# Routing of a mixture of experts behind an attention: smaller steps, another share of them per unit, and the last eight units as one group

## The chip, the core and the metric

The kernel runs on one core of one Trainium2 chip. TensorE (PE in the profile) multiplies matrices, VectorE (DVE), ScalarE (ACT) and GpSimd (POOL) work on tiles in SBUF and PSUM, and SyncE (SP) starts most of the DMAs. Each engine works off its own instructions in the order in which the program wrote them, and waits on semaphores for the others. The metric is the device time of one execution in microseconds.

## The reference, cut to what matters

An mLSTM-like attention over 4 batches, 8 heads, 768 positions and head size 40 gives 3072 rows of 320 numbers. A router picks two of eight experts for each row, and each expert is two matrix products with a maximum between them.

```python
x = attn_out.transpose(0, 2, 1, 3).reshape(3072, 320)
noisy = x @ w_gate + log1p(exp(x @ w_noise)) * noise
top2 = argpartition(-noisy, 2, axis=1)[:, :2]
w = exp(top2_l - top2_l.max()); w /= w.sum() + 1e-9
for e in range(8):
    for k in range(2):
        mask = top2[:, k] == e
        out[mask] += w[mask, k, None] * (maximum(x[mask] @ w1[e], 0) @ w2[e])
```

## The kernel before, in words

**The attention.** The time axis is cut in chunks of 64. A unit is one chunk of two batches with all heads, so there are 24 units (`NU`) of 128 rows. The main loop writes unit after unit by hand, with parts of the neighbours between: at the top the DMAs (`load_unit(i + 3)`, `keep_rows(i - 1)`, which stores the rows of the unit before, `gate_move`, a piece of the first expert's weights), then `k_part(i + 1)` and `p_part(i + 1)` (kd and p, two products on VectorE), `c_part(i)` and `o_part(i)` (TensorE: the state "st" and the output "o"), `e_part(i + 2)`, `f_part(i)` (VectorE: three steps dn and then tm, which read the bank "o"; GpSimd: xr, the unit's rows), logits and transposes of the units before (`l_part`, `t_part`), `s_part(i + 2)` and `sig_part(i + 1)` (ScalarE). There is one bank "o", so the next `o_part` waits for tm. xr also reads the output gate in the unit's input buffer, of which there are four, so SP's load of unit i + 3 waits for GpSimd's xr of unit i - 1.

**The routing.** Four units make a group (`GROUPS`). `g_part(g)` is a generator which writes one group's routing in small steps: logits with noise (two activations on ScalarE between), maxima and their indices (mx, mi), one-hot rows (oh), counts (m, base), then it asks for ranks (`want`), which TensorE adds up with three small products in `r_part`, and turns rank and expert into a place in a table. The place is written as two factors, oa (which of 56 columns) and ob (which of 128 rows), one ob per unit and choice; a burst of matmuls oa by ob in `b_part` adds the tokens' numbers to the table TBL. `decode` reads token numbers out of it, and `gather` fetches rows by them with indirect DMAs that GpSimd issues. Two small tables go on beside: WTS (weights of the two choices, stored behind the rows by a DMA on SP, `sent`) and OVM (for the case that an expert gets too many tokens, which these inputs don't reach).

**How the steps are shared out.** `fill(n)` writes the next n steps of the first group in the queue `routing`; a step that has to wait for another engine ends the fill. RATE gives three steps behind p and five at the unit's end (five and eight from unit 16), and `f_part` calls `fill` once behind each dn. `act()` writes the activations that the routing asked for.

**The first expert.** Its first tokens (places 0 to 511) come from units 0 to 15 alone: as soon as the bursts of four groups are done, the first 4 columns are decoded and four gathers start, beside unit 23. W1 of expert 0 is split in a high and a low half in the attention (`split_w1`: ScalarE w1h, VectorE w1l, line L142) at units 8, 10, ... 18. After the units, `mm1(0, 0, f)` makes eight first products of 512 tokens (banks s0, s1, e in turn; ScalarE hh and VectorE hlo empty each), with w2's split beside (w2h on ScalarE, w2l on GpSimd) and sixteen stores of zeros to the output (`wipe`). `push()` writes all the routing steps that can be written; the ranks and bursts of the last two groups stand between the products: ranks behind f = 0, a burst behind f = 3, ranks behind f = 5. Then `mm2` makes the second products of four tiles of 128 tokens, eight steps of three matmuls each; behind the sixth step of the first tile stand the last burst, the decode of the whole table and seven gathers, three of them for the rest of expert 0, whose transposes (L734) follow the four tiles. The experts 1 to 7 follow, TensorE's work throughout.

Of the kernel before, what the change touches and what calls it, by code (L numbers as in the profile page):

```python
# [8 lines left out]
FR = mybir.dt.float32r  # L9
# [12 lines left out]
NU = 2 * NCH  # L22
# [10 lines left out]
GROUPS = tuple((u, 4) for u in range(0, 24, 4))  # L33
GOF = {u: g for g, (u0, n) in enumerate(GROUPS) for u in range(u0, u0 + n)}
NB = 4

RATE = ((16, (3, 5)), (NU, (5, 8)))
# [14 lines left out]
C_ID, C_TRI, C_ONE, C_I8, C_TOK, C_N, C_SGN, C_VAC, C_END = 0, 128, 256, 384, 392, 416, 544, 592, 648  # L52


def at(plan, i):

    return next(v for end, v in plan if i < end)
# [3 lines left out]
def build(ctx, tc, qk, vk, fi, noise, wgn, w1, w2, cst, ce, out):  # L61
# [403 lines left out]
    acc, bump = {}, {}  # L465
# [6 lines left out]
    OB = rt.tile([128, 8, 128], FR, name="ob", bufs=1)  # L472
    OA = rt.tile([128, 8, NE * TC], FR, name="oa", bufs=1)

    def g_part(g):
# [39 lines left out]
        for j in range(nb):  # L515
            V.max(mx[:, j, :], nl[:, j, :])
            yield
        for j in range(nb):
            V.max_index(mi[:, j, :], mx[:, j, :], nl[:, j, :])
            yield  # L520
# [5 lines left out]
        yield  # L526
        oh4 = sm("oh", [128, nb, 2, NE])
        i8 = cs[:, None, None, C_I8:C_I8 + 8].to_broadcast([128, nb, 2, NE])
        V.tensor_tensor(oh4, i8, e12[:, :, :, None].to_broadcast([128, nb, 2, NE]), op=OP.is_equal)
        yield  # L530

        m = sm("m", [128, NE, nb + 1], BF)
        V.tensor_add(m[:, :, 1:].rearrange("p e u -> p u e"), oh4[:, :, 0], oh4[:, :, 1])
        if u0 == 0:
            V.memset(m[:, :, 0], 0.0)
# [9 lines left out]
        V.tensor_scalar(dd, d, 1.0, 1e-9, op0=OP.add, op1=OP.add)  # L545
# [4 lines left out]
        wt = WTS[:, u0:u0 + nb, 0:2]  # L550
        V.reciprocal(wt[:, :, 0], dd)
        yield
        V.tensor_mul(wt[:, :, 1], d, wt[:, :, 0])
# [20 lines left out]
        r = sm("r", [128, nb, 2])  # L574
        V.tensor_reduce(f(r), oh4.rearrange("p u k e -> p (u k) e"), AX.X, OP.add)
        yield
        ov = sm("ov", [128, nb, 2])
        ix = rt.tile([128, 2 * nb], I32, name=f"ix{u0}", bufs=1)
        V.tensor_scalar(ov, r, float(BLK), None, op0=OP.is_ge)
        V.scalar_tensor_tensor(r, e12, float(BLK), r, op0=OP.mult, op1=OP.add)  # L580
        yield
        V.scalar_tensor_tensor(ix, f(ov), 1e6, f(r), op0=OP.mult, op1=OP.add)
        V.tensor_mul(OVM[:, u0:u0 + nb, 2:4], wt, ov)
# [6 lines left out]
        V.scalar_tensor_tensor(bi, ai, -128.0, ix, op0=OP.mult, op1=OP.add)  # L590
# [575 lines left out]
```

## Time and profile before

| what | value |
|---|---|
| median of 3 runs | 584.05 us (583.41 to 586.16) |
| the profiled execution | 586.08 us, its span 584.2 us |
| busy: PE, DVE, ACT, POOL | 553.9, 360.8, 254.7, 217.2 us |
| mean granted TensorE clock | 0.948 |
| first product of the first expert | at 164.05 us |
| transposes of its second part | at 202.20 us |

A row of the timeline gives start, length, engine, source line, operation, output and inputs with their shape, the number of merged instructions, and in brackets how long the engine idled before it and what released it. Where several instructions are merged the length runs from the first one's start to the last one's end. A row of the windows gives busy times and counts of each engine in a stretch.

### The profile page before, as it was taken

The page shows a single profiled execution, that of the slowest core. Times are in us where ns is not written, and L with a number is a line of the kernel's source. Part 1 is how long each engine was busy: PE and PEld are TensorE (multiplying, and loading weights), DVE is VectorE, ACT ScalarE, POOL GpSimd, SP SyncE. Part 2 cuts the span into 40 slices and gives each one's busy share as a digit, 9 for nine tenths or more (in the row PEclk, how much of TensorE's full clock was granted, in tenths as well). Part 3 has the DMA queues.
Part 4 walks back from the last instruction along what each step waited for, and adds up shares of the span by engine and source line. Part 5 has one row for each costly group of instructions (what it writes and reads, how often), then busy time and mean ns, then how long its engine had stood idle before and what let it go on. Part 6 is the DMA issues. An engine that isn't in the chain of part 4 may idle for free.

```text
span 584.2 us, 13335 instructions
## 1 busy us (share of the span) xinstructions
PE 553.9 (95%) x5157; PEld 506.1 (87%) x5158; DVE 360.8 (62%) x990; ACT 254.7 (44%) x621; POOL 217.2 (37%) x276
## 2 busy tenths in 40 slices
PE   7899979898898999999999999999999999999995
PEld 3687878787776998899899999989989998998995
DVE  8899977898879147663565466356446636645511
ACT  6687848565424234541452254145235315513500
POOL 7355532111423464424604522460451344142043
PEclk9699969796778989999999999999999999999998
DMA  5888875675235956326426442632643343332024
GB/s 142 205 224 220 214 204 145 185 186 166 80 116 186 313 97 140 91 83 148 92 90 146 63 131 43 138 84 90 148 82 116 93 78 82 98 45 24 2 28 48
DMA packets 41060, 71.08 MB, mean 122 GB/s; under 512 B 8761, under 2 KB 30478, under 8 KB 40992
## 3 DMA queue, kind: packets, MB, share of 16 engines
q1 hardware_dynamic: 29632, 51.20, 30.3%
q0 software_dynamic: 11360, 18.98, 19.2%
q8 instruction: 42, 0.69, 0.5%
q14 instruction: 26, 0.21, 0.1%
HBM read 52.73 MB, written 17.73 MB: 121 GB/s over the span
## 4 chain that ended last, share of the span: by engine, by line
PE 70%; DVE 6%; ACT 3%; issue 2%; another core or an unknown queue 1%; DMA 1%; POOL 0%; POOLq 0%; DVEq 0%; ACTq 0%
PE s L871 21%; PE e L871 11%; PE st L890 5%; PE st L889 5%; PE st L891 5%; PE o L891 4%; PE o L890 4%; PE o L889 4%; PE s L734 3%; PE o L365 1%; PE o L898 1%; PE o L897 1%; DVE ob L600 1%; DVE p L342 1%
## 5 line engine op out<-in xcount | busy, mean ns | idle before, releaser
L915 POOL DMA_INDIRECT y_out<-y,tok x56 | 87.1, 1556 | 220.1 <-DVE y L905 219.3
L871 PE MATMUL s<-xh,w1h 128*128 128x512 f32 (+1 forms) x255 | 77.5, 359 | 1.8 <-DVE xh L738 1.2
L877 DVE SCALAR_TENSOR_TENSOR hlo<-s,hh 128x512 fp32r<-128x512 f32 (+1 forms) x85 | 47.4, 558 | 39.8 <-ACT hh L876 37.6
L736 ACT ACTIVATE xh<-s 128x384 fp32r<-128x384 f32 (+1 forms) x56 | 25.6, 470 | 105.3 <-PE s L734 104.6
L704 POOL DMA_INDIRECT xg<-rows,tok x56 | 57.4, 1024 | 25.3 <-issue 18.0
L876 ACT ACTIVATE hh<-s 128x512 fp32r<-128x512 f32 (+1 forms) x85 | 41.8, 492 | 49.2 <-PE s L871 41.2
L871 PE MATMUL s<-xh,w1l 128*128 128x512 f32 (+1 forms) x255 | 63.2, 357 | 0.0
L889 PE MATMUL st<-w2h,hh 128*128 128x320 f32 x184 | 58.3, 317 | 0.0
L890 PE MATMUL st<-w2l,hh 128*128 128x320 f32 x184 | 57.3, 312 | 0.0
L891 PE MATMUL st<-w2h,hlo 128*128 128x320 f32 x184 | 57.0, 310 | 0.0
L379 POOL TENSOR_TENSOR xr<-tm,vk 128x320 f32<-128x320 f32 x24 | 22.3, 928 | 86.2 <-DVE tm L378 13.2
L889 PE MATMUL o<-w2h,hh 128*128 128x320 f32 x168 | 53.2, 317 | 0.0
L871 PEld LDWEIGHTS s<-xh,w1h 128*128 128x128 f32 x255 | 46.5, 191 | 7.5 <-ACT xh L736 2.3
L890 PE MATMUL o<-w2l,hh 128*128 128x320 f32 x168 | 52.3, 312 | 0.0
L891 PE MATMUL o<-w2h,hlo 128*128 128x320 f32 x168 | 52.1, 310 | 0.2 <-DVE hlo L877 0.2
L871 PEld LDWEIGHTS s<-xh,w1l 128*128 128x128 f32 x255 | 45.7, 193 | 5.5
L871 PE MATMUL s<-xl,w1h 128*128 128x512 f32 (+1 forms) x170 | 46.9, 358 | 0.5 <-DVE xl L737 0.5
L142 DVE TENSOR_TENSOR w1l<-raw,w1h 128x512 fp32r<-128x512 f32 (+1 forms) x48 | 33.2, 692 | 12.9 <-ACT w1h L141 12.2
L871 PE MATMUL e<-xh,w1h 128*128 128x320 f32 (+1 forms) x129 | 39.0, 357 | 0.2 <-DVE ht L880 0.2
L365 PE MATMUL o<-vk,p 128*64 128x41 f32 (+2 forms) x768 | 29.9, 242 | 9.1 <-issue 3.1
L328 PE MATMUL s<-qk 64*64 64x64 f32 x768 | 37.2, 238 | 0.8 <-DVE hl L208 0.7
L737 DVE TENSOR_TENSOR xl<-s,xh 128x256 fp32r<-128x256 f32 (+1 forms) x56 | 22.6, 404 | 24.4 <-ACT xh L736 24.2
(200 smaller groups left out, 1347.3 us busy)
## 6 DMA issues: line engine op xcount, KB each, us to landing
vk<-vk_in SPq DMA_DIRECT2D x48, 242.0 KB
raw<-w_in SPq DMA_DIRECT2D x7, 1280.0 KB
qk<-qk_in SPq DMA_DIRECT2D x48, 160.0 KB
raw<-w_in SPq DMA_DIRECT2D x7, 1024.0 KB
y_out<-zrow SPq DMA_DIRECT2D x15, 320.0 KB
raw<-w_in SPq DMA_DIRECT2D x18, 256.0 KB
rows<-xr POOLq DMA_DIRECT2D x12, 160.0 KB
rows<-xr SPq DMA_DIRECT2D x12, 160.0 KB
```

The source lines that it names most:

```text
L142: lo.tensor_sub(W1L[n, k, s], RAW1[n, k, s], W1H[n, k, s].bitcast(F32))
L328: T.matmul(SQ[u][:, p][half[p], h, :], q[r, 1, h, :], q[r, 0, h, :], start=True, stop=True)
L365: T.matmul(OQ[u][half[p], h, :], PP[u][n, p, h, :], VK[u % 4][p][n, h * 41:h * 41 + 41], start=True, stop=True)
L704: P.indirect_dma_start(out=XG[0:rows_of(t), t], out_offset=None, in_=XD[0:n], in_offset=bass.IndirectOffsetOnAxis(ap=token(e, t), axis=0), ...
L736: A.activation(XH[:, :, c], ps[:, :, 0:n], AF.Copy)
L871: T.matmul(ps[:, 0:n], l, r, start=i == 0, stop=i == len(ops) - 1)
L876: A.activation(HH[:, f, c], ps[:, 0:m], AF.Relu)
L877: V.scalar_tensor_tensor(HLO[:, f, c], ps[:, 0:m], 0.0, HH[:, f, c].bitcast(F32), op0=OP.max, op1=OP.subtract)
L889: T.matmul(ps, HH[:, j, c], W2H[:, j], start=j == 0, stop=False)
L890: T.matmul(ps, HH[:, j, c], W2L[:, j], start=False, stop=False)
L891: T.matmul(ps, HLO[:, j, c], W2H[:, j], start=False, stop=j == 7)
L915: st = P.indirect_dma_start(out=out, out_offset=bass.IndirectOffsetOnAxis(ap=token(e, t), axis=0), in_=y[0:n], in_offset=None, compute_op= ...
```

## The change

The groups become four of four units and one of eight (units 16 to 23). `fill` no longer counts steps but the time that the program's author expects of them: a step costs what it yields (0.19 us if nothing), a unit's end fills up to `SHARE` = 1.8 us, the places behind p and dn take one short step each, and the steps oa and ob, marked "long", are written at the unit's end alone. `k_part(i + 2)` moves from the top of the next unit to this one's end, between two fills. The low half of expert 0's W1 goes from VectorE to GpSimd. In the routing, VectorE loses ov, two steps of ix and a product for OVM, since the experts' numbers are put into the table's columns as 32 times the expert (`C_COL`), so that rank and expert are one whole number; GpSimd takes d, dd, the copy e12, the second weight, and five small steps for OVM.

`push()` goes. The group of eight is routed by `beside`, once behind each first product from f = 1 on (1.2 us each) and behind each step of the second products (0.5 us each) until the table is whole. The core of the diff:

```diff
-GROUPS = tuple((u, 4) for u in range(0, 24, 4))
+GROUPS = ((0, 4), (4, 4), (8, 4), (12, 4), (16, 8))
-RATE = ((16, (3, 5)), (NU, (5, 8)))
+STEP, SHARE = 0.19, 1.8
...
-        V.tensor_sub(d, mx[:, :, 1], mx[:, :, 0])
-        e12 = OVM[:, u0:u0 + nb, 0:2]
-        V.tensor_copy(e12, mi[:, :, 0:2])
+        P.tensor_sub(d, mx[:, :, 1], mx[:, :, 0])
...
-        V.tensor_scalar(dd, d, 1.0, 1e-9, op0=OP.add, op1=OP.add)
+        P.tensor_scalar(dd, d, 1.0, 1e-9, op0=OP.add, op1=OP.add)
+        e12 = OVM[:, u0:u0 + nb, 0:2]
+        P.tensor_copy(e12, mi[:, :, 0:2])
...
-        V.tensor_mul(wt[:, :, 1], d, wt[:, :, 0])
+        P.tensor_mul(wt[:, :, 1], d, wt[:, :, 0])
...
-        V.tensor_scalar(ov, r, float(BLK), None, op0=OP.is_ge)
-        V.scalar_tensor_tensor(r, e12, float(BLK), r, op0=OP.mult, op1=OP.add)
-        V.scalar_tensor_tensor(ix, f(ov), 1e6, f(r), op0=OP.mult, op1=OP.add)
-        V.tensor_mul(OVM[:, u0:u0 + nb, 2:4], wt, ov)
-        V.tensor_scalar(ai, ix, 7, None, op0=OP.arith_shift_right)
+        V.tensor_scalar(ai, f(r), 7, None, op0=OP.arith_shift_right)
+        P.tensor_scalar(ov, e12, -4096.0, None, op0=OP.mult)
+        P.tensor_copy(rf, r)
+        P.tensor_add(ov, ov, rf)
+        P.tensor_scalar(ov, ov, float(BLK), None, op0=OP.is_ge)
+        P.tensor_mul(OVM[:, u0:u0 + nb, 2:4], wt, ov)
...
-    pre1 = split_w1(V)
+    pre1 = split_w1(P)
...
+    def fill(upto=0.2, much=True):
+        end = spent[0] + upto
+        for g in list(routing):
+            while spent[0] + 0.05 < end and (much or g not in long):
+                long.discard(g)
+                r = next(g, "end")
...
-        fill(f2)
+        if i + 2 < NU:
+            k_part(i + 2)
+        fill(SHARE - spent[0])
...
+    def beside(upto):
+        if want:
+            ranks()
+        elif bursts:
+            burst()
+        fill(upto)
+        act()
+        tell()
...
-        if f == 3 and done[0] < GROUPS[-1][0]:
-            burst()
-        if f == 5:
-            ranks()
-            push()
+        if f:
+            beside(1.2)
...
-            if t == 0 and next(step) == 5:
-                burst()
-                decode(E0S[1] // 128, NE * TC)
-                gather(0, 1)
-                gather(1, ts=tiles(0, 0))
+            if not whole_table():
+                beside(0.5)
+                if whole_table():
+                    decode(E0S[1] // 128, NE * TC)
+                    gather(0, 1)
+                    gather(1, ts=tiles(0, 0))
```

The first place is VectorE in the attention, where the first group's table factors are written. Before, in unit 10, oa and all eight ob stand between p and tm:

```order
L342 TENSOR_TENSOR p<-s,w 128x1024
L590 SCALAR_TENSOR_TENSOR bi_1326<-ai_1311,ix_1306 128x8
L596 TENSOR_TENSOR oa<-cs,ai_1311 128x448
L600 TENSOR_SCALAR ob<-cs,bi_1326 128x128 x4
L370 TENSOR_SCALAR dn<-o 128x8
L600 TENSOR_SCALAR ob<-cs,bi_1326 128x128 x2
L372 SCALAR_TENSOR_TENSOR dn<-o,dn 128x8
L600 TENSOR_SCALAR ob<-cs,bi_1326 128x128 x2
L374 RECIPROCAL dn<-dn 128x8
L378 TENSOR_TENSOR tm<-o,dn 128x320
```

After the change they stand one unit earlier, in two units:

```order
L596 TENSOR_TENSOR oa<-cs,ai_1210 128x448
L602 TENSOR_SCALAR ob<-cs,bi_1219 128x128 x2
L331 TENSOR_TENSOR kd<-vk_104,w 128x640
L337 TENSOR_TENSOR p<-s,w 128x1024
L365 TENSOR_SCALAR dn<-o 128x8
L367 SCALAR_TENSOR_TENSOR dn<-o,dn 128x8
L369 RECIPROCAL dn<-dn 128x8
L373 TENSOR_TENSOR tm<-o,dn 128x320
L602 TENSOR_SCALAR ob<-cs,bi_1219 128x128 x6
L337 TENSOR_TENSOR p<-s,w 128x1024
```

Nothing of them is left between p and tm; they stand behind tm, ahead of the next kd and p.

The second place is GpSimd's queue at unit 8. Before, xr, the clearing of a buffer (xg) and the store of the rows are all there is:

```order
L379 TENSOR_TENSOR xr<-tm,vk_104 128x320
L818 MEMSET xg 128x336
L382 DMA rows<-xr 128x320
L379 TENSOR_TENSOR xr<-tm,vk_105 128x320
L818 MEMSET xg 128x336
```

After, the second weight (wts), the five steps for OVM and the split of W1 are among them:

```order
L550 TENSOR_TENSOR wts<-d_1091,wts 128x4
L374 TENSOR_TENSOR xr<-tm,vk_102 128x320
L581 TENSOR_SCALAR ov_1212<-ovm 128x8
L583 CAST rf_1214<-r_1208 128x8
L584 TENSOR_TENSOR ov_1212<-ov_1212,rf_1214 128x8
L585 TENSOR_SCALAR ov_1212<-ov_1212 128x8
L586 TENSOR_TENSOR ovm<-wts,ov_1212 128x4x2
L137 TENSOR_TENSOR w1l<-raw_113,w1h 128x512
L834 MEMSET xg 128x336
L377 DMA rows<-xr 128x320
L374 TENSOR_TENSOR xr<-tm,vk_103 128x320
```

What stands ahead of the next xr has grown by seven steps, one of them as wide as a weight's half.

The third place is TensorE in the first expert. Before, the ranks of the last group stand between two of the first products:

```order
L871 MATMUL s_3076<-xh,w1h 128x512
L419 LDWEIGHTS tri
L419 MATMUL o<-m_3009,tri 128x32
L420 LDWEIGHTS ones
L420 MATMUL o<-base_4_3012,ones 128x32
```

After, the ranks of the group of eight stand behind all eight products, and its burst of sixteen behind two steps of the second tile's second products:

```order
L414 MATMUL o<-m_3010,tri 128x64
L415 LDWEIGHTS ones
L415 MATMUL o<-base_8_3013,ones 128x64
L416 LDWEIGHTS ones
L416 MATMUL o<-base_8_3013,ones 128x8
L909 MATMUL s_3077<-w2h,hh 128x320
```

```order
L910 MATMUL s_3120<-w2l,hh 128x320
L911 MATMUL s_3120<-w2h,hlo 128x320
L425 MATMUL o<-oa,ob 128x56 x16
L909 MATMUL s_3120<-w2h,hh 128x320
L910 MATMUL s_3120<-w2l,hh 128x320
```

The first products follow each other without routing's matmuls between them, and the ten steps between ranks and burst are what stands beside VectorE's work on the table factors.

More of the change, by code (lines that the diff above doesn't have):

```diff
@@ L50 @@
 W1LD, W1AT, W2AT = 6, 8, 19
-C_ID, C_TRI, C_ONE, C_I8, C_TOK, C_N, C_SGN, C_VAC, C_END = 0, 128, 256, 384, 392, 416, 544, 592, 648
-def at(plan, i):
-    return next(v for end, v in plan if i < end)
+C_ID, C_TRI, C_ONE, C_I8, C_TOK, C_N, C_SGN, C_VAC, C_COL, C_END = 0, 128, 256, 384, 392, 416, 544, 592, 648, 704
 @with_exitstack
@@ L463, in lc_part @@
             w[4] = True
-    acc, bump = {}, {}
+    acc, bump, ranked = {}, {}, set()
     anew = {}
@@ L516, in g_part @@
             V.max(mx[:, j, :], nl[:, j, :])
[L517 removed]
+            yield 0.1
         for j in range(nb):
             V.max_index(mi[:, j, :], mx[:, j, :], nl[:, j, :])
[L520 removed]
+            yield 0.15
         d = sm("d", [128, nb])
[L522 to L524 removed]
+        P.tensor_sub(d, mx[:, :, 1], mx[:, :, 0])
         acts.append((d, d, AF.Exp))
[L526 removed]
         oh4 = sm("oh", [128, nb, 2, NE])
         i8 = cs[:, None, None, C_I8:C_I8 + 8].to_broadcast([128, nb, 2, NE])
[L529 removed]
+        V.tensor_tensor(oh4, i8, mi[:, :, 0:2, None].to_broadcast([128, nb, 2, NE]), op=OP.is_equal)
         yield
+        while g and g - 1 not in ranked:
+            yield "wait"
         m = sm("m", [128, NE, nb + 1], BF)
@@ L534, in g_part @@
         if u0 == 0:
-            V.memset(m[:, :, 0], 0.0)
+            V.tensor_scalar(m[:, :, 0], cs[:, C_I8:C_I8 + 8], 32.0, None, op0=OP.mult)
         else:
@@ L620, in build @@
     routing = []
-    def fill(n=1):
-        for _ in range(n):
-            if not routing:
-                return
-            try:
-                r = next(routing[0])
-                if r == "wait":
-                    return
-            except StopIteration:
-                routing.pop(0)
+    spent, long = [0.0], set()
+    def fill(upto=0.2, much=True):
[4 more added lines that the diff above has]
+                r = next(g, "end")
+                if r == "end":
+                    routing.remove(g)
+                if r in ("wait", "end"):
+                    break
+                if r == "long":
+                    long.add(g)
+                else:
+                    spent[0] += r or STEP
     def act():
@@ L784, in build @@
             p_part(i + 1)
-        fill(f1)
+        fill(0.2, False)
         if i + 2 < NU:
@@ L836, in burst, with whole_table @@
         bc_part(t, b_part(t), True)
-    def push():
-        while True:
-            fill(100)
-            if not acts:
-                tell()
-                return
-            act()
+    def beside(upto):
[4 more added lines that the diff above has]
+        fill(upto)
+        act()
+        tell()
+    def whole_table():
+        return done[0] == NU and not routing
     keep_rows(NU - 1)
```

48 lines of the change are left out of this document (25 added, 23 removed).

## The prediction

> **What bounds the kernel now.** I read the page's head first, then the engines' busy time by stretch, and then the timeline of VectorE (DVE) and TensorE (PE) where TensorE idles. The program computes the attention in 24 units and then runs the experts; the change lies in the units and in the first expert.
>
> ```profile
> span 584.2 us, 13335 instructions
> 40.00:50.00 10.00, 9.88 (x223) 8.73 (x224) 9.52 (x21) 7.69 (x19) 4.88 (x7) 1.00 0.85 232
> 60.00:150.00 90.00, 81.39 (x1582) 72.71 (x1578) 74.95 (x258) 58.01 (x149) 23.74 (x38) 0.85 0.67 179
> 280.00:580.00 300.00, 297.42 (x1830) 280.46 (x1828) 153.66 (x353) 107.47 (x263) 107.25 (x120) 1.00 0.39 83
> ```
>
> In a windows row the busy times of PE, its weight load, DVE, ACT and POOL follow the length, then granted clock, DMA share and GB/s. From 40 to 50 TensorE is busy 9.88 of 10 us at full clock; from 60 to 150 its clock averages 0.85. From 280 on TensorE is busy 297.42 of 300 at full clock: the experts behind the first are its own work, and nothing in the diff touches them.
>
> The last VectorE step of a unit is tm, which empties the only bank "o". Four of them give the pace:
>
> ```profile
> 43.05 0.49 DVE L378 TENSOR_TENSOR tm<-o,dn 128x320 f32<-128x320 f32 x1
> 43.45 0.27 DVE L201 TENSOR_TENSOR xg<-raw,xg 64x128 f32<-64x128 f32 x1
> 45.04 0.47 DVE L208 SCALAR_TENSOR_TENSOR hl<-hl,raw,xg 64x256 fp32r<-64x256 f32 x1
> 48.00 0.49 DVE L378 TENSOR_TENSOR tm<-o,dn 128x320 f32<-128x320 f32 x1
> 58.90 0.49 DVE L378 TENSOR_TENSOR tm<-o,dn 128x320 f32<-128x320 f32 x1
> 153.00 0.49 DVE L378 TENSOR_TENSOR tm<-o,dn 128x320 f32<-128x320 f32 x1
> ```
>
> Unit 5 takes 48.00 - 43.05 = 4.95 us although VectorE does gate steps from 43.45 to about 45.45, that is 2.0 us beside the unit's own steps: TensorE sets that pace. Units 8 to 22 take 153.00 - 58.90 = 94.1 us, 6.27 each. The routing is what they have more. Unit 10 shows how it costs:
>
> ```profile
> 72.75 0.62 DVE L596 TENSOR_TENSOR oa<-cs,ai 128x448 fp32r<-128x448 f32 x1
> 73.29 1.11 DVE L600 TENSOR_SCALAR ob<-cs,bi 128x128 fp32r<-128x128 f32 x4
> 75.79 0.49 DVE L378 TENSOR_TENSOR tm<-o,dn 128x320 f32<-128x320 f32 x1
> 76.38 1.94 PE L365 MATMUL o<-vk,p 104*64 104x41 f32 x32 [3.09 <-issue]
> ...
> 80.00:85.00 5.00, 4.98 (x48) 4.36 (x49) 3.69 (x13) 2.55 (x8) 2.52 (x5) 0.50 0.57 175
> ```
>
> The eight ob and the oa stand ahead of tm, TensorE has no free bank "o" and idles 3.09 us, and then its clock is 0.50 in 80 to 85: the wait is paid a second time as slow matmuls. Six times VectorE also does its half of the weight split, and five of them its queue waits for ScalarE's half:
>
> ```profile
> L142 DVE TENSOR_TENSOR w1l<-raw,w1h x6: 689/692/693, 65.7 to 128.5; 128x512 fp32r<-128x512 f32 x4, 64x512 fp32r<-64x512 f32 x2
> ...
>   ACT w1h L141: 5.7, 5
> ```
>
> **The change, part by part.** (1) The w1l split of expert 0 goes to GpSimd (POOL). VectorE loses 6 x 0.69 = 4.1 us of work and 5.7 of waiting, 9.8 in all, between 65 and 129. What waits instead is POOL, with the next xr behind it.
>
> One group's ranks, table factors and ob, the last of before, stand in the trace so, and then a product's hlo:
>
> ```profile
> 183.04 0.22 DVE L559 TENSOR_SCALAR rk<-rk,bump 128x4 f32<-128x4 f32 x1
> 184.06 0.17 DVE L580 SCALAR_TENSOR_TENSOR r<-ovm,r 128x8 f32<-128x8 f32 x1
> 184.26 0.17 DVE L582 SCALAR_TENSOR_TENSOR ix<-ov,r 128x8 int32<-128x8 f32 x1
> 184.75 0.62 DVE L596 TENSOR_TENSOR oa<-cs,ai 128x448 fp32r<-128x448 f32 x1
> 185.28 2.84 DVE L600 TENSOR_SCALAR ob<-cs,bi 128x128 fp32r<-128x128 f32 x8
> 188.49 0.68 DVE L877 SCALAR_TENSOR_TENSOR hlo<-s,hh 128x512 fp32r<-128x512 f32 x1
> ```
>
> (2) The lighter routing. VectorE drops ov, the r and ix steps and the OVM product, and hands d, dd, the copy of e12 and the second weight to POOL: eight small steps less per group, 0.2 us each (184.06 to 184.26), 1.6 us for each of four groups. The 9.8 and the 1.6 are not added up: the pace of the units is worked out from what is left on VectorE.
>
> (3) The portions. In after's order the work of a group falls into four units: A logits (eight small steps, 1.7, and one maximum, 0.1), B indices (about 0.9), C ranks and indices (183.04 to 184.75 without the three dropped steps and the bump of the first row: 0.9), oa (to 185.28, 0.5) and two ob (0.5, at 1.11 for four), together 1.9, D six ob (1.6). All stand between tm and the next kd. A step on POOL can hold VectorE meanwhile:
>
> ```profile
> 81.98 0.91 POOL L379 TENSOR_TENSOR xr<-tm,vk 128x320 f32<-128x320 f32 x1 [3.80 <-DMA vk<-vk_in]
> 82.20 0.74 DVE L508 TENSOR_TENSOR ln<-ln,nzt 128x32 f32<-128x32 f32 x1
> 82.97 0.19 DVE L511 TENSOR_TENSOR nl<-ln,lg 128x32 f32<-128x32 f32 x1
> ...
> 189.86 0.97 PE L430 MATMUL o<-oa,ob 128*128 128x56 f32 x8
> ```
>
> The ln takes 0.74 where its like takes 0.19, and ends with xr. I add 0.6 us to each unit: A 2.4, B 1.5, C 2.5, D 2.2. Unit 5 hid 2.0; the excess is 0.4, 0, 0.5, 0.2. So A 5.35, B 4.95, C 5.45, D 5.15, and the burst of eight matmuls adds the 0.97 us of its row to one of the four: 21.9 for four units, 5.5 each, 82.2 for fifteen. TensorE's waits fall under a microsecond, so I give its clock no cost.
>
> ```profile
> L379 POOL TENSOR_TENSOR xr<-tm,vk 128x320 f32<-128x320 f32 x24 | 22.3, 928 | 86.2 <-DVE tm L378 13.2
> L718 POOL TENSOR_TENSOR w2l<-raw,w2h x8: 862/888/1318, 168.9 to 188.5; 128x320 fp32r<-128x320 f32 x8
> ```
>
> (4) What POOL takes on: w1l, and eight small steps a group. Its price for 128x512 is not in the trace; 128x320 takes 0.93 (xr) and 0.89 (w2l), so 1.4 by size. Where it falls in p and tm it holds nobody, where it falls in two-input steps it holds VectorE for all of it: between 0 and 6 x 1.4 = 8.4 us, and I take 2.5, nearer to the lower end, since ScalarE's half ends late in the unit, where VectorE is at p. Of the 32 small steps I count half at 0.1 us, 1.5. A gain is excluded here: this work was not on POOL before.
>
> So the fifteen units: 82.2 + 2.5 + 1.5 = 86.2 against 94.1: **7.9 us less**. kd's move ahead of the second fill changes nothing I can see; its cover is the wait for w. Between unit 22 and the first product of the expert stand the table, the decode and four gathers in both (153.00 to 164.05, 11.05): no change, 0.5 either way.
>
> ```profile
> 164.05 1.22 PE L871 MATMUL s<-xh,w1h 128*128 128x512 f32 x2 [0.58 <-ACT xh L736]
> 170.77 0.70 PE L871 MATMUL s<-xh,w1h 128*128 128x512 f32 x2
> 181.97 0.18 PE L419 MATMUL o<-m,tri 128*128 128x32 bf16 x1 [2.71 <-DVE tbl L437]
> 185.40 0.63 PE L871 MATMUL e<-xh,w1h 128*128 128x512 f32 x2
> 187.25 0.30 PE L889 MATMUL s<-w2h,hh 128*128 128x320 f32 x1
> 187.69 0.30 PE L889 MATMUL s<-w2h,hh 128*128 128x320 f32 x1
> 202.20 1.14 PE L734 MATMUL s<-cs,xg 128*128 128x128 f32 x9
> ```
>
> (5) The first expert's first products. Now they take 187.25 - 164.05 = 23.2 us. At full clock one is 187.25 - 185.40 = 1.85. After keeps the first two, with transposes and logits (170.77 - 164.05 = 6.7), and has no rank or burst among the other six: 6 x 1.85 = 11.1, so 17.8, **5.4 less**, provided VectorE keeps up: it gets about 1.2 us of routing and 0.6 of hlo per product of 1.85.
>
> (6) Behind them it gives back. The rank of eight units follows the last product, the burst stands behind ten steps of the second products and needs sixteen ob.
>
> VectorE needs, after the last hlo (about 2 us behind the last product: hh, the hlo of 0.68 and their turns), ranks and indices 1.1 (183.04 to 184.75 without the three dropped steps), oa twice 0.53 and twice eight ob of 2.2 (2.84 with a POOL step among them): 2 + 1.1 + 1.1 + 4.4 = 8.6 us, to 9.4 with POOL. TensorE is there after 10 x (187.69 - 187.25) = 4.4 us. It waits 4.2 to 5.0, and the matmuls of the burst trickle in that wait, so that before's 0.97 falls away. After the wait of 2.71 before the rank at 181.97 the next product took until 185.40, 3.4 instead of 1.85, 1.5 more; I count the same here. Together 4.6 - 1.0 + 1.5 = **5.1 given back**, 4.6 being the middle, since POOL has five steps of the group there. The gathers then start about 10.5 us behind the last product; 202.20 - 187.25 = 15.0 us was the way to the transposes and is now 20, so they stay hidden. The sixteen zero stores leave SP before the weights' store instead of behind it; nothing on the path waits for them.
>
> Sum: 7.9 + 5.4 - 5.1 = 8.2 us. The profiled execution took 586.08 (span 584.2 and 1.9 around it), 2.0 above the median of the runs shown, 584.05. Taken from the one it gives 577.9; the runs that are compared have the median, so 584.05 - 8.2 = 575.9, and I say 576.
>
> **The clock.** In 80 to 85 the clock is 0.50, more than 3.6 us after the wait of unit 10 ended at 76.38. The Trainium skill's "TensorE: Matmul & The Clock Gate", Part 1, has a gate look at windows of about 3.4 us, an idle one halving the clock and a busy one restoring it. The trace agrees with the half, not with the length: by that rule the wait in (6) would cost 1.7 us (an estimate from its window) instead of 1.5, and the sum would be 8.0.
>
> **The rivals.** *VectorE stops being late at all.* POOL's work falls beside p and tm, and every unit goes at 4.95 with one burst in four: 15 x 5.2 = 78 us, 16 less; with the first expert even, 568. For it: unit 5's row. Against it: the 0.74 above, once in nearly every unit. Chance 0.18.
>
> *POOL holds VectorE* (the other side):
>
> ```profile
> 52.41 0.97 POOL L269 MEMSET w1l<- 64x1024 f32 x1
> 54.08 0.89 POOL L379 TENSOR_TENSOR xr<-tm,vk 128x320 f32<-128x320 f32 x1
> 52.51 2.81 DVE L491 TENSOR_SCALAR t<-ue 128x32 f32<-128x32 f32 x1
> ```
>
> A step of 0.17 us lasts 2.81 there, until POOL's run of steps is over. After puts five small steps, w1l, a memset and xr on POOL, often in one run. If such a run costs VectorE 1.2 us more a unit than I counted, the fifteen units lose 18 us against my sum, TensorE's waits pass 2 us and the clock halves again: 584.05 - 8.2 + 18 = 594. It turns the gain into a loss from 0.55 us a unit. Against it: POOL is busy 23.74 of 90 us and waits between its steps. Chance 0.12. The Trainium skill, "SBUF — State Buffer", "Who interferes with whom", states the rule: one port pair is shared by VectorE and GpSimd and goes to one instruction at a time; a VectorE step with two SBUF inputs, or in a two-port mode, is fully blocked meanwhile. The trace agrees, in this fence and in that of (3). By that rule every w1l that meets such a step costs its 1.4, and if all did, the sum would be 8.2 - 5.9 = 2.3 us (an estimate, with the 1.4 of (4)).
>
> *The group of eight costs what the units gain.* VectorE falls behind in the first products (1.85 us each with 1.8 of work, POOL's w2l of 0.89 beside them), the burst comes 3 us later, and then the gathers come late for the transposes by as much: 584.05 - 8.2 + 6 = 582. Chance 0.17.
>
> **How the numbers follow.** My forecast, 571 to 581, has 0.53. The range takes in the first rival's 568 and below it the part where POOL is free and the wait in (6) short (565), and above it the third and the lower part of the second (587). About 0.5% (3 us) is what a measurement here can tell from no change: faster than 581.1 holds the forecast and the first rival, 0.71; the third, 0.17; slower 0.12.
>
> **What would show it.** Right: tm to tm at 5.4 to 5.9 from unit 8 to 22, no TensorE wait over 2 us there, clock near 1.0 from 60 to 150; first products in about 18 us; TensorE waiting 4 to 5 us for ob at the burst. Wrong: two-input VectorE steps of over 1 us beside POOL in most units; first products over 21 us; the transposes waiting for a gather; DMA waits for vk or qk as the units close up (the share was 0.85 at the pace of 4.95).

## The result, and the profile after

The changed kernel takes 576.04 us (median of five executions, 571.31 to 585.20), the kernel before 583.41 beside it (582.54 to 586.16). The ratio is 0.9847, with a 95% interval of 0.9808 to 0.9886: 1.5% faster. The ratio leaves out the slowest of the five executions, which took over 1.5% longer than the fastest. The forecast was 576, within 565 to 587. The executions of the changed kernel lie 14 us apart, those of before 3.6.

The execution that was profiled is the slowest of the five (585.20, span 583.3), so its profile stands 0.9 us from that of before and not 7.4. It shows where time came and went, and one reason for the scatter. First VectorE's tm of units 7 and 22, as they were shown of before, and windows over that stretch and two parts of it (after the length: busy time of PE, its weight load, DVE, ACT and POOL, then granted clock, DMA share and GB/s):

```profile
61.99 0.49 DVE L373 TENSOR_TENSOR tm<-o,dn 128x320 f32<-128x320 f32 x1
149.66 0.49 DVE L373 TENSOR_TENSOR tm<-o,dn 128x320 f32<-128x320 f32 x1
```

```profile
62.00:149.70 87.70, 84.39 (x1667) 74.67 (x1659) 74.73 (x230) 59.93 (x153) 45.07 (x80) 0.85 0.72 186
50.00:80.00 30.00, 27.43 (x527) 24.22 (x520) 25.12 (x74) 18.62 (x47) 19.98 (x37) 0.77 0.71 193
110.00:140.00 30.00, 28.20 (x626) 24.50 (x620) 28.53 (x95) 23.71 (x62) 13.81 (x22) 1.00 0.76 187
```

Over units 8 to 22 the kernel before has this row:

```profile
58.90:153.00 94.10, 84.70 (x1635) 75.47 (x1635) 78.88 (x275) 59.16 (x152) 24.20 (x38) 0.85 0.65 175
```

Units 8 to 22 take 87.67 us instead of 94.1. From 110 to 140, at full clock, VectorE is busy 28.53 of 30 us: it sets the pace there. From 50 to 80 it is busy only 25.12, TensorE 27.43, and the clock is 0.77: there the pace is that of slow matmuls. What stands ahead of that stretch is in the waits of TensorE and of ScalarE from 20 to 165 (total, times, longest) and in the rows of four engines:

```profile
PE e L298 <- ACT w L301: 6.2, 4, 2.5
...
ACT d L648 <- POOL d L517: 7.2, 4, 2.8
ACT ln L648 <- DVE t L486: 2.7, 1, 2.7
```

```profile
54.88 2.79 DVE L486 TENSOR_SCALAR t<-ue 128x32 f32<-128x32 f32 x1
54.77 0.97 POOL L264 MEMSET w1l<- 64x1024 f32 x1
57.24 0.39 POOL L834 MEMSET xg<- 128x336 f32 x1
57.71 0.23 ACT L648 ACTIVATE ln<-t 128x32 f32<-128x32 f32 x1 [2.65 <-DVE t L486]
60.75 0.79 PE L298 MATMUL e<-re,le 98*128 98x512 f32 x1 [2.54 <-ACT w L301]
```

VectorE's t lasts 2.79 us beside GpSimd's memsets, xr and xg, as it lasted 2.81 before. But now the routing's logarithm ln stands on ScalarE ahead of the three vk and of the next w; it waits 2.65 us for t, and TensorE waits 2.54 us for w. The exponential of d has the same place, and ScalarE waits four times for it, 7.2 us in all. The forecast had no TensorE wait over a microsecond and no clock cost here.

The row of before in which TensorE begins the second half of the first expert:

```profile
204.54 0.53 PE L871 MATMUL s<-xh,w1h 128*128 128x320 f32 x2 [1.20 <-DVE xh L738]
```

TensorE's rows in the first expert of the changed kernel: its first product, the first product of the second layer, the burst, the product behind it, and the first product of the second half:

```profile
160.80 1.22 PE L891 MATMUL s<-xh,w1h 128*128 128x512 f32 x2 [0.58 <-ACT xh L748]
179.40 0.39 PE L909 MATMUL s<-w2h,hh 128*128 128x320 f32 x1
184.04 4.18 PE L425 MATMUL o<-oa,ob 128*128 128x56 f32 x16
188.04 0.62 PE L909 MATMUL s<-w2h,hh 128*128 128x320 f32 x1
202.30 0.53 PE L891 MATMUL s<-xh,w1h 128*128 128x320 f32 x2 [0.87 <-DVE xh L750]
```

The first products take 179.40 - 160.80 = 18.6 us (before 23.2). The burst holds TensorE for 4.18 us, in which its sixteen matmuls trickle as the ob come, and behind it the matmuls run at half clock (0.62 and then 0.47 instead of 0.31). From 179.40 to the second half are 22.9 us, where before had 187.25 to 204.54, 17.3.

The profiled spans add up: 3.3 us by the end of unit 22 (153.00 - 149.66), 0.1 lost before the first product, 4.6 gained in the products, 5.6 lost up to the second half, 1.3 lost from there to the end (381.0 against 379.7): 0.9, the difference of 584.2 and 583.3. The loss at the end is in a stage that the forecast called untouched.

### The profile page after: what moved, and what is told of

Same layout as the page of the kernel before. It is cut to its first block, busy times and chain, and to the rows that moved or that the text cites. A ratio compares the mean times of both kernels' runs of the same rounds, so it can differ in the third digit from the quotient of the medians.

```text
span 583.3 us, 13303 instructions
## 1 busy us (share of the span) xinstructions
PE 559.1 (96%) x5155; PEld 507.1 (87%) x5155; DVE 351.3 (60%) x916; ACT 254.7 (44%) x617; POOL 243.0 (42%) x329
## 4 chain that ended last, share of the span: by engine, by line
PE 83%; DVE 6%; DMA 5%; issue 2%; ACT 2%; SPq 1%; POOL 1%; POOLq 0%; DVEq 0%
PE s L891 23%; PE e L891 12%; PE st L909 5%; PE st L910 5%; PE st L911 5%; PE o L909 4%; PE o L910 4%; PE o L911 4%; PE s L746 3%; PE s L323 3%; PE o L360 3%; DMA qk<-qk_in 2%; PE e L298 2%; PE st L351 2%; PE xt L405 1%
## 5 line engine op out<-in xcount | busy, mean ns | idle before, releaser
L323 PE MATMUL s<-qk 64*64 64x64 f32 x768 | 38.9, 245 | 0.1
L897 DVE SCALAR_TENSOR_TENSOR hlo<-e,hh 128x256 fp32r<-128x256 f32 (+1 forms) x43 | 23.8, 554 | 21.2 <-ACT hh L896 18.2
L925 DVE TENSOR_SCALAR y<-st,gw 128x320 f32<-128x320 f32 x23 | 12.7, 551 | 39.3 <-PE st L911 39.3
```

The lines of the kernel that those rows point to most:

```text
L323: T.matmul(SQ[u][:, p][half[p], h, :], q[r, 1, h, :], q[r, 0, h, :], start=True, stop=True)
L897: V.scalar_tensor_tensor(HLO[:, f, c], ps[:, 0:m], 0.0, HH[:, f, c].bitcast(F32), op0=OP.max, op1=OP.subtract)
```

## The experiments

Theory A is the forecast's: VectorE's load sets the units, and TensorE's clock is no part of it. Theory B is the rival formed from the profile: routing functions on ScalarE wait ahead of sigma and vk, TensorE waits behind them, its clock halves, and this gives part of VectorE's gain back, more in some executions than in others. The kernel before ran beside these kernels at 582.8 to 583.7 us (medians of 11 to 17 executions), and ratios are to that.

### The changed kernel again

> The changed kernel, unaltered, for a profile of an ordinary execution: the one shown came at 585.2 us, its other four at 571 to 579. Theory A (VectorE's load sets the units; TensorE's clock plays no part): units 8 to 22 take 86 to 87 us, as in the profile shown (87.7), the products of the first expert's second layer end about 8 us earlier than before, and the times scatter for no reason that the attention shows. Theory B (ScalarE's queue: exp(d) and the logarithm now stand ahead of sigma and vk, wait there for GpSimd's d or for a held VectorE step, and TensorE's waits of 1.4 to 2.5 us halve its clock for some 10 us): the time goes with the granted clock, about 2.5 us for each 0.003, and the faster profile has at least one half-clock stretch fewer between 50 and 110 us, with tm of unit 6 back at about 52 instead of 54.5.

577.85 us (571.15 to 583.45), ratio 0.9856 (0.9804 to 0.9907). Its profile is again that of the slowest execution; one with less disturbance comes with a later kernel. The times go with the clock, as theory B has it: 571.15 and 571.82 at 0.969 and 0.970, 577 to 579 at 0.955 to 0.964, 583.45 at 0.952. The price was set too high: 571.31 at 0.970 and 585.20 at 0.944, the ends of the first five executions, are 1.6 us for each 0.003.

### d back on VectorE

```diff
-        P.tensor_sub(d, mx[:, :, 1], mx[:, :, 0])
+        V.tensor_sub(d, mx[:, :, 1], mx[:, :, 0])
```

> The small step d (difference of the two best logits) of each group is back on VectorE, all else as changed. Theory A: five more VectorE steps of about 0.15 us, so 0 to 1 us slower than the changed kernel, scatter as before. Theory B: ScalarE's four waits for GpSimd's d (7.2 us in the profile shown, longest 2.8) fall to under 0.5 us each; TensorE's wait of 1.43 us at 91.7 goes; median 2 to 5 us below the changed kernel's and its runs closer together.

575.01 us (573.12 to 576.47), ratio 0.9848 (0.9815 to 0.9881). The runs lie closer together, but the median is not lower by what the intervals can tell, and ScalarE's longest wait for d is still 2.2 us: VectorE comes to it late as well. That GpSimd makes d is not the cause; where its exponential stands may be. One pair of rows is worth more than the time. TensorE's wait of unit 6 and the clock over 50 to 80, in this kernel:

```profile
58.42 0.55 PE L298 MATMUL e<-re,le 98*128 98x512 f32 x1 [2.57 <-ACT w L301]
```

```profile
50.00:80.00 30.00, 27.41 (x565) 24.02 (x566) 28.07 (x87) 21.65 (x56) 22.03 (x39) 0.94 0.81 209
```

The wait is the same as in the changed kernel (2.54, where the clock was 0.77); the clock loses a quarter as much.

### w1l back on VectorE

```diff
-    pre1 = split_w1(P)
+    pre1 = split_w1(V)
```

> The six steps w1l of the attention units are back on VectorE, all else as changed. Theory A (the prediction's first term): VectorE gets 4.1 us of work back and the wait for w1h with it, units 8 to 22 grow by 4 to 8 us, and so does the time. Theory B: VectorE is the bound only in part of the units; GpSimd loses six steps of 1.3 us that held d back, so the time grows by less, 0 to 3 us.

581.62 us (577.98 to 590.58), ratio 0.9966 (0.9938 to 0.9994). Without this one part nearly the whole gain is gone: 4 to 6 us by the medians, 6 to 7 by the ratios, which is theory A's 4 to 8. But a part of it comes with the clock. At a granted clock of 0.955 four executions take 580.8 to 582.0 us, and two of the changed kernel, repeated above, 578.6 and 579.0, so at one clock about 2.5 us are left, which is theory B's 0 to 3. Whether w1l on VectorE is also what lowers the clock more often was not tested. In the profile VectorE waits 0.4 us in all for w1h, not the 5.7 of the kernel before, so mostly the work came back. Units 8 to 22 take 86.9 us there, no longer than in the changed kernel's two profiles, which lost more to the clock; the price is read from the times alone.

### Two groups of four at the end

```diff
-GROUPS = ((0, 4), (4, 4), (8, 4), (12, 4), (16, 8))
+GROUPS = tuple((u, 4) for u in range(0, 24, 4))
...
-NB = 8
+NB = 4
```

> The last eight units are again two groups of four, with the lighter routing, the portions and w1l on GpSimd as changed. The prediction's sums: the burst behind the products waits for eight ob instead of sixteen (2.1 us less wait, and about 1 us less of halved clock), but a second set of small steps (about 8 us of VectorE) and a second burst beside the first expert's first layer: 1 us faster to 3 us slower than the changed kernel. The rival that the group of eight gives back what the units gain: 4 to 6 us faster than the changed kernel, nearly all of it between the last product and the next expert half's first layer.

576.14 us (574.81 to 579.43), ratio 0.9875 (0.9836 to 0.9913), not told apart from the changed kernel. The profile has both sides: the first products take 21.8 us (18.6 with the group of eight), the way from there to the second half 21.6 (22.9). So in these profiles the group of eight gains 3.2 us in the products and loses 1.3 behind them; in the times the two programs are not told apart.

### The routing functions behind vk

```diff
         fill(SHARE - spent[0])
-        act()
         if i + 1 < NU:
             sig_part(i + 1)
         if i + 2 < NU:
             k_part(i + 2)
+        act()
         fill(SHARE - spent[0])
```

> Only ScalarE's order differs from the changed kernel: the routing's logarithm and exponential stand behind sigma and the three vk of the same unit, as in the kernel before, and no longer ahead of them; every other engine has the same rows. Theory B (ScalarE's queue and the clock): the waits of 2.5 us at about 58 to 60 and 1.4 us at 85 to 92 for the gate's tanh w go or fall to about 1 us, no half-clock stretch of 10 us is left between 55 and 110, the median is 571 us or less and the runs lie within 3 us. Theory A (VectorE's load sets the units, the clock's chance is not tied to these waits): time and scatter as the changed kernel's, 571 to 583.

571.66 us (568.99 to 579.41), ratio 0.9812 (0.9778 to 0.9847); the interval overlaps the changed kernel's a little. TensorE's waits from 20 to 145, the row of the longest, and the clock in two windows:

```profile
PE e L298 <- ACT w L301: 2.9, 4, 1.2
PE o L360 <- DVE tm L373: 2.8, 4, 1.8
```

```profile
82.12 1.16 PE L360 MATMUL o<-vk,p 64*64 64x41 f32 x30 [1.75 <-DVE tm L373]
```

```profile
60.00:70.00 10.00, 9.78 (x225) 8.54 (x225) 9.59 (x27) 8.22 (x21) 9.07 (x19) 1.00 0.70 182
80.00:90.00 10.00, 8.22 (x139) 7.22 (x135) 9.44 (x35) 4.95 (x13) 7.06 (x16) 0.66 0.64 175
```

Theory B is right on the place: only ScalarE's order changed, the wait for w went from 2.5 to 1.2 us, and the clock from 60 to 70 is full. It is wrong that this was all: with VectorE now the late one, TensorE waits 1.75 us for tm at 82, the clock halves behind that, and the executions still lie 10 us apart, where theory B had them within 3.

### The burst two by two

```diff
-        elif bursts:
-            burst()
+        elif bursts or drip:
+            if not drip:
+                b = bursts.pop(0)
+                drip.extend([psum.tile([128, 512], F32, name="o"), b, 0])
+            t, b, j0 = drip
+            n = len(b[0])
+            for j in range(j0, j0 + 2):
+                T.matmul(t[:, LGC + 24:LGC + 24 + NE * TC], b[0][j], b[1][j], start=j == 0, stop=j == n - 1)
+            drip[2] += 2
+            if drip[2] == n:
+                bc_part(t, b, True)
+                drip.clear()
```

> The sixteen matmuls of the burst behind the first expert's products are spread: two behind each of eight steps of the second layer, where the changed kernel has all sixteen in one place. The prediction's term (the burst waits 4.2 to 5.0 us for its sixteen ob, and the clock halves behind it): both go, decode and gathers stay where they are (189 us in the profile shown), so the products end some 6 us earlier and the next transposes wait for the gathers only; 3 to 6 us faster than the changed kernel, from the first layer of the next half on. The rival that the gathers bound that place: the transposes stay at the gathers' landing and the time falls by under 1.5 us.

568.40 us (567.12 to 576.55), ratio 0.9750 (0.9724 to 0.9777): some 6 us below the changed kernel by the ratios, which have their intervals apart. TensorE's first product of the second layer, the first of the eight pairs, and the second half's first product:

```profile
170.27 0.40 PE L921 MATMUL s<-w2h,hh 128*128 128x320 f32 x1
174.92 0.46 PE L867 MATMUL o<-oa,ob 128*128 128x56 f32 x2
188.60 0.53 PE L903 MATMUL s<-xh,w1h 128*128 128x320 f32 x2 [0.87 <-DVE xh L750]
```

No pair waits, the clock stays whole, and 170.27 to 188.60 are 18.3 us instead of 22.9. The gathers are not late: the same 0.87 us stands before the second half. Up to the burst this program is the changed kernel, row for row, so it also gives the attention with little disturbance:

```profile
64.47 0.49 DVE L373 TENSOR_TENSOR tm<-o,dn 128x320 f32<-128x320 f32 x1
141.32 0.49 DVE L373 TENSOR_TENSOR tm<-o,dn 128x320 f32<-128x320 f32 x1
```

```profile
64.50:141.30 76.80, 74.39 (x1651) 65.94 (x1647) 72.75 (x229) 59.73 (x152) 44.71 (x80) 0.98 0.80 211
20.00:58.00 38.00, 37.89 (x699) 32.95 (x699) 30.12 (x68) 23.68 (x55) 17.00 (x25) 0.73 0.73 188
```

Units 8 to 22 take 76.85 us, 5.1 a unit, with VectorE busy 72.75. This execution had its slow clock earlier: 0.73 from 20 to 58, which is 20.5 us at half clock.

### 288 bytes, and the memsets earlier

```diff
-    tri = keep.tile([128, 128], BF, name="tri")
+    tri = keep.tile([128, 272], BF, name="tri")[:, 0:128]
...
     def constants():
-        P.memset(W1L[0:64, 2].bitcast(F32), 0.0)
         V.tensor_copy(toki, cs[:, C_TOK:C_TOK + NU])
-        P.memset(zrow, 0.0)
-        P.memset(TBL, 0.0)
-        P.memset(WTS, 0.0)
...
+        if i == 2:
+            P.memset(W1L[0:64, 2].bitcast(F32), 0.0)
+        if i == 3:
+            P.memset(zrow, 0.0)
+            P.memset(TBL, 0.0)
+            P.memset(WTS, 0.0)
```

> The changed kernel with two edits that show at different places. First, every tile behind the constants lies 288 bytes further, so that the first layer's weights stand at the same place within 512 bytes as in the kernel before (25824, 25536 in the changed kernel, 25312 before). In the profiles of all changed kernels so far the eight groups of 512-wide products in the experts' first layer take 1.867 us each where before's take 1.815. Theory of the address: they return to 1.815, which is 8 x 0.05 x 7 experts = about 3 us of the span. If the address plays no part they stay at 1.867. Second, the four memsets of the seventh unit stand in units 2 and 3: theory B expects the held VectorE step (2.8 us at 54.9) and TensorE's wait of 2.5 us behind it to go, with the half clock of 60 to 70; the wait for the second d, 1.4 us, stays. Together 571 us or less; under theory A 574 to 579.

570.44 us (564.99 to 572.62), ratio 0.9811 (0.9784 to 0.9837). The group of TensorE's 512-wide products of xh and w1h from 250 to 540 us (busy, mean ns), with the rows in which the first of eight such products and the first 320-wide one of the second expert begin, of the changed kernel and then of this one:

```profile
L891 PE MATMUL s<-xh,w1h 128*128 128x512 f32 x91 | 31.5, 400 | 0.0
```

```profile
276.26 0.50 PE L891 MATMUL s<-xh,w1h 128*128 128x512 f32 x1
291.30 0.46 PE L891 MATMUL s<-xh,w1h 128*128 128x320 f32 x2
```

```profile
L893 PE MATMUL s<-xh,w1h 128*128 128x512 f32 x96 | 32.6, 394 | 0.0
```

```profile
258.52 0.74 PE L893 MATMUL s<-xh,w1h 128*128 128x512 f32 x2
273.16 0.45 PE L893 MATMUL s<-xh,w1h 128*128 128x320 f32 x2
```

```profile
50.00:80.00 30.00, 28.55 (x639) 25.05 (x637) 28.63 (x99) 21.98 (x57) 21.28 (x39) 1.00 0.89 229
```

The eight products take 291.30 - 276.26 = 15.04 us in the changed kernel and 273.16 - 258.52 = 14.64 here. The kernel before has the 394 as well. The address theory holds: the change widened the constants by 56 columns, 224 bytes, every tile behind them moved, and the 512-wide products became 2.7% slower, with no instruction of that stage changed; 0.40 us for each of seven experts is 2.8. The second edit worked as well: the clock from 50 to 80 is 1.00, and TensorE's longest wait there is 1.24 us.

### The kernel before with w1l on GpSimd alone

```diff
-    pre1 = split_w1(V)
+    pre1 = split_w1(P)
```

> The kernel before with one part of the change alone: the six w1l steps of the attention units on GpSimd. Theory A (the prediction's first term, 4.1 us of work and 5.7 us of waiting taken from VectorE, which sets the units there): units 8 to 22 shrink by 3 to 6 us and the time by as much. Rival: without the lighter routing VectorE's late units are those that route, w1l stands in others, and the time falls by under 2 us.

575.62 us (572.42 to 579.04), ratio 0.9881 (0.9835 to 0.9928). VectorE's tm of units 7 and 22, and the windows over that stretch:

```profile
59.94 0.49 DVE L378 TENSOR_TENSOR tm<-o,dn 128x320 f32<-128x320 f32 x1
144.36 0.49 DVE L378 TENSOR_TENSOR tm<-o,dn 128x320 f32<-128x320 f32 x1
```

```profile
59.90:144.40 84.50, 79.06 (x1638) 70.19 (x1637) 76.64 (x271) 59.40 (x153) 32.48 (x44) 0.92 0.73 195
```

The units take 84.4 us, 9.7 less, and the time falls by 7: theory A, above its own range. Of the 9.7, 2.2 are VectorE's busy time (76.64 instead of 78.88) and 7.4 are time in which it was idle. The clock is 0.92 instead of 0.85 in this stretch, but the fall of the time is not the clock's: at a mean of 0.956 and 0.957 this kernel takes 574.9 and 576.4 us, the kernel before at 0.955 580.5 to 584.0. One line of the change makes most of what the whole change shows.

### All four edits, and three variants of it

The four edits that gained above (order on ScalarE, burst two by two, 288 bytes, memsets) together:

> The changed kernel with all four edits that gained: routing functions behind sigma and vk on ScalarE, the burst's sixteen matmuls two by two behind eight steps of the second layer, the memsets in units 2 and 3, and the tiles behind the constants 288 bytes further. If the four are worth what their places showed and lie at different places: the burst 6 us, the 512-wide products 3 us, one half-clock stretch 2 to 5 us against the changed kernel's 576 to 578: 562 to 567 us. If the units fall back on VectorE's load whatever stands on ScalarE (theory A), the first edit and the memsets add nothing and it lands at 567 to 570.

565.86 us (564.29 to 570.68), ratio 0.9714 (0.9664 to 0.9765), within the first expectation: faster than both kernels, 10 us below the changed one.

The same with the 288 bytes behind the weights, so that hh and hlo move and w1h and w1l stand where the changed kernel has them:

```diff
-    RAW2 = m2.tile([128, 8, DM], F32, name="raw2")
+    RAW2 = m2.tile([128, 8 * DM + 72], F32, name="raw2")[:, 0:8 * DM].rearrange("p (j c) -> p j c", j=8)
```

> The same as the version with all four edits, but the 288 bytes lie behind the weights of the first layer: w1h and w1l stand where the changed kernel has them (25536, 37824), hh and hlo 288 bytes further than there. If the place of the weights sets the pace of the 512-wide products, they are back at 394 and 400 ns by the profile's rows (389 and 394 with the weights moved) and the time is about 3 us above the other. If it is the place of hh and hlo, which ScalarE and VectorE write while the products run, they stay at 389 and 394.

566.50 us (566.02 to 567.63), ratio 0.9717 (0.9661 to 0.9773). Its 512-wide products of xh and w1h, then VectorE's y of two tiles of its second layer, and two in the version before it:

```profile
L905 PE MATMUL s<-xh,w1h 128*128 128x512 f32 x96 | 33.2, 400 | 0.0
```

```profile
448.05 0.55 DVE L939 TENSOR_SCALAR y<-o,gw 128x320 f32<-128x320 f32 x1 [1.44 <-PE o L925]
451.85 0.55 DVE L939 TENSOR_SCALAR y<-st,gw 128x320 f32<-128x320 f32 x1 [2.17 <-PE st L925]
```

```profile
446.98 0.55 DVE L939 TENSOR_SCALAR y<-o,gw 128x320 f32<-128x320 f32 x1 [1.50 <-PE o L925]
450.84 0.55 DVE L939 TENSOR_SCALAR y<-st,gw 128x320 f32<-128x320 f32 x1 [2.22 <-PE st L925]
```

The weights' place sets the pace of the first layer: the 400 is back. The time hardly shows it, since here the second layer became faster: a tile of it takes 451.85 - 448.05 = 3.80 us, against 450.84 - 446.98 = 3.86 in the version before and 3.90 in the kernel before (its fifth expert, y at 417.40 and 421.30). So the places of both layers' operands matter; which distance is good was not found.

The nine small routing steps that the change gave to GpSimd, back on VectorE (nine lines `P.` to `V.`):

> The version with all four edits, and the nine small routing steps of each group that the change gave to GpSimd (d, its sum, the experts' numbers, the second weight and the five of the overflow list) back on VectorE. The prediction's term (lighter routing spares VectorE 1.6 us a group, and VectorE sets the units): 1.3 to 2 us for each of the three groups inside units 8 to 22, 4 to 6 us slower than the version with all four edits. The rival that these steps fit into VectorE's gaps, or that GpSimd holds VectorE by as much as it spares: 0 to 2 us.

574.66 us (572.88 to 576.29), ratio 0.9854 (0.9809 to 0.9899), 8.8 us slower, more than either expected. Windows over units 8 to 22 of this kernel, and of the version with all four edits:

```profile
58.70:146.70 88.00, 77.91 (x1638) 68.47 (x1636) 83.13 (x266) 59.41 (x152) 30.78 (x44) 0.95 0.73 193
```

```profile
58.30:136.80 78.50, 73.70 (x1638) 64.79 (x1636) 75.50 (x230) 59.72 (x155) 44.02 (x80) 1.00 0.80 215
```

VectorE gets 36 more steps (nine for each of four groups, where the expectation counted three groups) and 7.6 us more work, 0.21 a step, and the units grow by 9.5. A part of the rest goes with the clock, 0.95 instead of 1.00. VectorE is the bound there.

The version with all four edits, but six groups of four:

> The version with all four edits, but the last eight units again two groups of four: the fifth group's burst of eight stands whole beside the first layer's products, the sixth group's eight matmuls two by two behind four steps of the second layer. The rival of the prediction (the group of eight gives back what the units gain) with the burst's price taken away: no more than 1 us between the two, either way. The prediction's sum (the group of eight spares one set of small steps and one selection, which shorten the first expert's products by 3 to 4 us): 2 to 4 us slower than the version with the group of eight, with the products at 21 to 22 us instead of 17.7 to 19.4.

576.46 us (575.32 to 578.19), ratio 0.9890 (0.9858 to 0.9922), 10.6 us slower. TensorE's first products of both layers and of the second half:

```profile
150.98 0.80 PE L907 MATMUL s<-xh,w1h 128*128 128x512 f32 x1 [0.58 <-ACT xh L744]
174.85 0.47 PE L925 MATMUL s<-w2h,hh 128*128 128x320 f32 x1
196.24 0.53 PE L907 MATMUL s<-xh,w1h 128*128 128x320 f32 x2 [3.10 <-DVE xh L746]
```

The first product comes 3.1 us later, the products take 23.9 us (19.4 with the group of eight), and from there to the second half it is 21.4 instead of 18.0, with a wait of 3.10 instead of 0.88 before it: VectorE's xh stands behind ScalarE's, which comes late for a reason that was not followed up. So here the group of eight is worth more than either theory gave it. The burst's price is not gone from the comparison, though: the fifth group's burst still stands whole between the first products, TensorE waits 1.7 us in it for ob, and 6.8 us at half clock lie between 169 and 177.

## Why the prediction was right, and where it was not

**The time was right; of the sum behind it three terms were right, and errors of both signs in the others nearly cancel.** That 576.04 came so near to 576 is luck. By its own steps:

- *(1) w1l, 9.8 us off VectorE:* right for the kernel before. Alone it shortened the units by 9.7 us, and with it taken back nearly the whole gain was gone from the times. In the changed kernel the two parts of the term are not both there: with w1l on VectorE again, its wait for w1h is 0.4 us and not 5.7.
- *(2) lighter routing, 1.6 us a group:* the mechanism right, the size near. Putting back the nine steps that GpSimd took cost VectorE 7.6 us of work in four groups, 1.9 a group, and the time 8.8. Four of the nine are among the eight steps of the term; the other five, for OVM, stand in place of four that VectorE had.
- *(3) "5.5 each, 82.2 for fifteen", with (4) 86.2:* wrong. With the clock nearly whole the units take 76.85 us. Fifteen units at 4.95 are 74.25 us; on top of that the sum put 12.0 us for routing's excess, the bursts, 0.6 us of hold in every unit and GpSimd's new work (eight small steps a group, where the change has nine), and 2.6 were measured. VectorE worked 78.88 of 94.1 us before and 72.75 of 76.85 here: of 17 us gained, 6 are work and 11 are idle time. w1l alone took away 7.4 us of idle time, as the kernel before with w1l on GpSimd shows. How the rest divides between the smaller steps, their places and the clock (0.85 before, 0.92 with w1l moved alone, 0.98 here) was not separated. The first rival (VectorE stops being late at all, 78 us) had the number, but not the reason: VectorE is still the bound, busy 95%, and 7.6 us more of work lengthen the units.
- *"TensorE's waits fall under a microsecond, so I give its clock no cost":* wrong, and this is what hid the error above: in the profiled execution, at a clock of 0.85, the units take 87.67 us, near the 86.2. The added act() ahead of sigma and vk put routing functions in front of w, and the held step and the late d reached TensorE through ScalarE. With its order as before, or without the memsets there, the wait of 2.5 us halved and the half clock from 60 to 70 was gone.
- *(5) first products 17.8:* right within 1.6 us: 17.7 to 19.4 in the profiles with the group of eight.
- *(6) 5.1 given back at the burst:* right. It was 5.6, with a wait of 4.18 against "4.2 to 5.0". Spreading the burst took 4.6 of it away.
- *"nothing in the diff touches them"*, of the experts behind the first: wrong by 1.3 us in the profiles. The diff widens a table, and the tiles behind it moved: the first layer's products cost 2.8 us more, of which the second layer, whose operands moved too, gives a part back (3.86 us a tile instead of 3.90).

Together, from the attention of the execution with little disturbance: 11.7 by the end of unit 22, in spite of 5.6 us lost before unit 8, 5.3 in the products, 5.6 and 1.3 lost: about 10 us, against 8.2 forecast and 7.4 measured.

**The rivals.** *POOL holds VectorE* fell: with twice the instructions on GpSimd (80 and 38 in the windows of units 8 to 22), VectorE's busy time in the units went down. One step shows that the hold is real, though. In the kernel with ScalarE's order as before, VectorE's ln and GpSimd's w1l start together:

```profile
77.45 1.30 DVE L503 TENSOR_TENSOR ln<-ln,nzt 128x32 f32<-128x32 f32 x1
77.43 1.27 POOL L137 TENSOR_TENSOR w1l<-raw,w1h 128x512 fp32r<-128x512 f32 x1 [0.29 <-ACT w1h L136]
```

The ln takes 1.30 where its like takes 0.19, and w1l 1.27, where 1.4 was estimated. It happens seldom: three small steps of VectorE last over a microsecond in units 8 to 22 of that kernel, and none in those of the kernel with the burst two by two. *The group of eight costs what the units gain* fell: its mechanism was late products and late gathers, but the products gain 4.6 us and the second half waits 0.87 us for xh, not longer than before (1.20). What the group of eight gives back, it gives back at the burst, as (6) has it, and most of that only because the burst stands in one piece.

**What stays open.** What decides how long the clock stays halved, on which the scatter hangs, and which distance between the operands is the good one. Both are narrowed in the last section. Open too is how much of the units' gain is due to the smaller steps and how much to the clock.

## What to carry to other kernels

When work leaves the engine that is late, recompute the idle time too, not only its steps: of 17 us gained in these units 11 were idle time, 7.4 of them with one step that had waited in VectorE's queue for ScalarE. A small function put ahead of a critical one in an in-order queue costs whatever its own input is late by, so look at what stands behind it. Before calling a stage untouched, see whether a tile ahead of it changed its size, and spread a row of matmuls that wait one by one for an engine over the products beside them.

## What the hardware showed that was not expected

**The half clock comes in pieces of one length, and how many follow a wait is not set by the wait.** From the windows: (1 - clock) x 2 x length is the time at half clock. After the wait of 2.5 us in unit 6 it is 13.8 us in the changed kernel (0.77 of 30 us), 13.8 in its repeat, 3.6 with d on VectorE and 3.6 with six groups of four (0.94). After a wait of 1.75 us for tm, windows from 76 to 96 of the version with all four edits, then of the one with the weights in their old place:

```profile
76.00:96.00 20.00, 17.90 (x389) 15.45 (x388) 19.20 (x60) 13.95 (x37) 12.07 (x22) 1.00 0.75 206
```

```profile
76.00:96.00 20.00, 18.11 (x345) 16.01 (x344) 18.42 (x58) 13.10 (x33) 12.22 (x22) 0.83 0.89 221
```

That is none and 6.8 us; with the order of ScalarE alone it was 6.8, with six groups of four 3.6. All are near 0, 1, 2 or 4 times 3.4. Read in windows of 1 us, every stretch of half clock that lies whole between 15 and 210 us, in all fourteen profiles, is 3.4, 6.8, 10.2, 13.7, 17.1 or 20.5 us, that is 1 to 6 times 3.4. A wait of 1.42 or 1.43 us for the second w shows the same: 13.7 us at half clock behind it in the changed kernel, none with the burst two by two and none with the memsets earlier. The Trainium skill's "TensorE: Matmul & The Clock Gate", Part 1, has windows of about 3.4 us that run freely and are not tied to the work; the runs agree with that length as a unit, which corrects the prediction's "not with the length"; but the clock halves here behind waits of 1.4 to 3.1 us, under one window, and up to four windows in a row stay slow while TensorE is busy (six in the profile with the burst two by two: 0.73 of 38 us, with TensorE busy 37.89). What decides their number was not settled; that a freely running window makes it a matter of chance fits, but was not tested. Between 571.31 us at clock 0.970 and 585.20 at 0.944 lie 31 us more of half clock, about nine such pieces, at 1.5 us each: the scatter goes with them.

**The place of a matmul's operands in the memory of a partition changes its pace.** With w1h at byte 25536 of a partition a 512-wide product of xh and w1h takes 400 ns by its row, at 25312 (before) and at 25824 it takes 394; these are the places in the built programs. xh did not move. For the seven experts behind the first it makes 2.8 us.
